# New places for the steps of the first third in a table-ordered kernel: attention front, its border to the second MLP pass, and that pass's first and last weight groups

## The chip, the cores and the metric

The kernel runs on one core of one Trainium2 chip. The metric is the device time of a run in microseconds (us), as the median of several runs. Five engines take part, each with its own instruction stream in program order: PE (TensorE: matrix multiplications and transposes), DVE (VectorE), ACT (ScalarE), POOL (GpSimd) and SP (SyncE, which here only issues DMA transfers). An engine starts an instruction when the one before it on the same engine allows it and when the semaphores named in its wait have reached their counts. ACT issues a few transfers too, and each of them stands in ACT's stream like any other instruction.

## The reference

```python
def phi(x):                                  # q and k: 4 batches, 8 heads, 576 rows, 64 columns
    proj = np.einsum('bhsd,df->bhsf', x, w_phi)              # w_phi: 64 x 128
    proj = proj - np.max(np.abs(proj), axis=-1, keepdims=True)
    return np.concatenate([np.exp(proj), np.exp(-proj)], axis=-1)
kv, z = einsum(k_p, v), sum(k_p)
x = (q_p @ kv) / (q_p @ z + 1e-06)           # linear attention, laid out as 2304 x 512
h = np.maximum(x @ moe_w_in, 0.0);  x = h * h @ moe_w_out              # 512 -> 2048 -> 512
p = probs / (probs.sum(-1, keepdims=True) + 1e-9)
out = sum over e of p[:, e:e+1] * (np.maximum(x @ w1[e], 0) @ w2[e])    # 4 experts, 512 -> 1024 -> 512
```

Everything is float32.

## The kernel before

**Arithmetic.** Most float32 products are made of three matmuls on a high part and a low part of each operand (`hi*hi + hi*lo + lo*hi`). So most operands need two more instructions: a copy that makes the high part (`copy`, L78 on ACT, L80 on DVE or POOL) and a subtraction that makes the low part (`sub`, L83 on DVE or POOL).

**Stages.** The attention works on 16 pairs of heads, `Pair(b, c)` with batch b and c from 0 to 3; P12 below is `Pair(1, 2)`. A pair loads q and k in three parts (`lqk`), transposes them on PE (`t_pe`), splits them (`t_hi` on ACT, `t_lo` on DVE), multiplies them with the split `w_phi` (`project`), shifts and exponentiates (`shift`, `exp_k`, `q_exp`), and forms the numerator (`num_pe` on PE, `num_out` on ACT). The denominator then makes two round trips through DRAM, all of them issued by SP: `den_put`, `den_get`, then `invert` on DVE, then `rec_put`, `rec_get`, and `divide` on DVE. The numerator's buffer exists once, so the next pair's `num_out` waits for this pair's `divide`.

Every product with `w_phi` needs the tile `wd`, which holds `w_phi` twice: `load_wd` loads one half by SP (L99) and the other by ACT (L100), and the step `split` makes `wd_h` and `wd_l` on DVE.

While the attention runs, the first MLP runs for batches 0 and 1, in `Unit` steps: U6b0 is weight group 6 of 8 on batch 0, with `hidden` (x @ w_in, L482), `relu`, `square`, the split of the result (`g_hi`, `g_lo`), and `out` 0 to 3 (L528, six matmuls each), whose results are summed by `add` (L536, DVE). `Matrix` steps turn the packed weights into float32 between them (`load`, `widen...`, `store`, `hi`, `lo`).

Then comes the border. Batches 2 and 3 take their MLP in a form with seven half-size products in place of eight. Its operands are sums of blocks of x: `Operands.load` (L1230, SP) fetches the x that P33, the last pair, has just stored (`put_x`, L387), and `Operands.sum` makes T3, T1, T2 and T4 on DVE (L83, 128x1024). `Rest` holds the rows left over from all batches; `Rest.make` splits them (ACT L78, DVE L83), and `RestUnit.hidden` (L1547) multiplies them. `PairUnit.product` (L1517) runs the seven products. Then follow the passes of the last stage, the mixture of experts, whose first weights are made in the last MLP group (575 to 625 us).

**Order.** Nothing in the loops decides the order. The table `PLACES` has one number for each call of each step; the function `at` takes the numbers of a step one after the other and sorts the calls by them, and this order is the order of the program on all engines:

```python
t = UNTIL * next(places["" if x is None else type(x).__name__, fn.__name__]) / STEPS
plan.append((t, len(plan), fn, args))
...
for _, _, fn, args in sorted(plan, key=lambda x: x[:2]):
    fn(*args)
```

For the pair steps with several calls the numbers run over the 16 pairs, and within a pair over the calls (for `t_pe` to `q_exp` these are columns 0 to 3, column 8, and columns 4 to 7 of nine).

Of the kernel before, what the change touches and what calls it, by code (L numbers as in the profile page):

```python
# [21 lines left out]
def fused_kernel(  # L22
# [515 lines left out]
    def new_x2(b):  # L538
# [12 lines left out]
            34, 1, 31,  # L551
        ),
        ("", "load_wd"): (
            2,
        ),
        ("", "split"): (
            3,
        ),
        ("Pair", "lqk"): (
            0, 13, 4, 25, 21, 50, 37, 41, 69, 71, 76, 80, 173, 168, 136, 185, 198, 145, 243, 233, 272, 294, 360, 297,  # L560
            388, 419, 367, 407, 573, 518, 508, 639, 583, 678, 618, 737, 828, 806, 855, 869, 964, 954, 916, 1182,
            1042, 1136, 1088, 1220,
        ),
        ("Pair", "lv"): (
            36, 35, 38, 78, 79, 53, 89, 43, 57, 154, 133, 195, 216, 237, 267, 271, 338, 290, 362, 372, 318, 425, 382,
            399, 549, 434, 569, 614, 501, 648, 740, 747, 780, 794, 887, 862, 1011, 1015, 944, 1123, 1106, 1195, 1298,
            951, 1301, 1189, 1200, 1023,
        ),
        ("Pair", "t_pe"): (
            5, 8, 14, 28, 56, 23, 40, 94, 92, 129, 115, 140, 179, 202, 201, 225, 261, 260, 278, 331, 329, 340, 353,  # L570
            395, 429, 397, 477, 458, 562, 574, 582, 626, 690, 686, 777, 772, 829, 913, 844, 930, 1052, 1062, 1127,
            1069, 1213, 1231, 1315, 1296,
        ),
        ("Pair", "t_hi"): (
            6, 9, 17, 42, 70, 29, 73, 97, 122, 135, 118, 142, 180, 208, 211, 230, 268, 275, 298, 332, 336, 341, 354,
            403, 440, 398, 480, 500, 566, 581, 594, 627, 693, 687, 779, 818, 858, 914, 845, 961, 1053, 1066, 1129,
            1087, 1214, 1232, 1319, 1304,
        ),
        ("Pair", "t_lo"): (
            7, 10, 20, 47, 72, 44, 87, 102, 126, 143, 119, 149, 193, 210, 212, 239, 269, 279, 310, 334, 337, 344,  # L580
            396, 414, 442, 411, 493, 516, 576, 592, 604, 628, 717, 688, 789, 819, 859, 920, 846, 1012, 1054, 1086,
            1145, 1125, 1259, 1233, 1352, 1305,
        ),
        ("Pair", "project"): (
            11, 16, 22, 48, 91, 63, 96, 116, 137, 161, 124, 172, 194, 221, 224, 253, 276, 292, 313, 335, 351, 377,
            402, 424, 445, 428, 522, 563, 577, 593, 653, 691, 718, 773, 821, 840, 878, 943, 980, 1019, 1075, 1094,
            1159, 1216, 1276, 1310, 1356, 1393,
        ),
        ("Pair", "shift"): (
            12, 26, 39, 49, 100, 64, 105, 127, 146, 165, 132, 184, 197, 238, 235, 258, 277, 293, 333, 342, 375, 409,  # L590
            413, 439, 483, 450, 543, 564, 589, 624, 677, 695, 739, 792, 822, 841, 927, 968, 997, 1073, 1084, 1140,
            1191, 1242, 1291, 1318, 1383, 1400,
        ),
        ("Pair", "exp_k"): (
            19, 27, 45, 67, 106, 101, 123, 128, 153, 183, 141, 189, 215, 244, 262, 282, 321, 339, 348, 343, 389, 447,
            415, 455, 506, 533, 555, 600, 590, 643, 745, 722, 752, 797, 871, 867, 966, 998, 1020, 1074, 1099, 1170,
            1253, 1267, 1306, 1360, 1401, 1412,
        ),
        ("Pair", "q_pe"): (
            18, 30, 54, 74, 107, 103, 144, 130, 160, 187, 156, 218, 214, 250, 273, 289, 285, 311, 347, 358, 386, 417,  # L600
            423, 469, 519, 536, 559, 605, 651, 655, 746, 714, 767, 823, 868, 910, 971, 977, 1007, 1133, 1144, 1143,
            1245, 1272, 1328, 1341, 1385, 1411,
        ),
        ("Pair", "q_exp"): (
            24, 32, 55, 81, 108, 111, 147, 169, 175, 188, 205, 223, 248, 257, 274, 304, 327, 328, 391, 380, 390, 418,
            463, 471, 521, 540, 572, 610, 652, 673, 750, 734, 775, 850, 870, 918, 972, 994, 1034, 1134, 1164, 1156,
            1246, 1273, 1333, 1357, 1408, 1419,
        ),
# [12 lines left out]
        ),  # L621
        ("Pair", "divide"): (
            157, 151, 219, 217, 283, 280, 349, 346, 421, 416, 468, 466, 539, 537, 607, 609, 704, 700, 847, 879, 1017,
            1006, 1155, 1161, 1275, 1280, 1363, 1365, 1436, 1435, 1489, 1490,
        ),
        ("Pair", "x_hi"): (
            200, 301, 314, 400, 443, 490, 591, 612,
        ),
        ("Pair", "x_lo"): (
            226, 326, 404, 460, 453, 561, 619, 623,  # L630
        ),
        ("Pair", "put_rest"): (
            220, 305, 352, 379, 454, 567, 662, 712, 778, 1137, 1103, 1201, 1418, 1406, 1439, 1501,
        ),
        ("Pair", "put_x"): (
            768, 1083, 1219, 1217, 1309, 1416, 1438, 1515,
        ),
        ("Matrix", "load"): (
            213, 15, 68, 361, 467, 492, 150, 596, 685, 731, 587, 835, 743, 813, 784, 946, 889, 978, 936, 1078, 1102,
            1190, 1013, 1205, 1209, 1324, 1149, 1355, 1295, 1404, 1392, 1493,  # L640
        ),
        ("Matrix", "widen"): (
            231, 33, 104, 401, 475, 534, 308, 646, 701, 732, 601, 836, 757, 890, 785, 981, 922, 1028, 952, 1079,
            1116, 1192, 1043, 1252, 1261, 1354, 1163, 1386, 1311, 1461, 1417, 1495,
        ),
        ("Matrix", "widen_power"): (
            284, 51, 174, 427, 498, 535, 309, 658, 707, 736, 602, 853, 764, 897, 790, 982, 923, 1029, 953, 1095,
            1117, 1193, 1048, 1254, 1262, 1359, 1180, 1394, 1312, 1464, 1426, 1508,
        ),
# [1364 lines left out]
```

## Time and profile before

| | before |
|---|---|
| runs shown | 1344.47, 1345.91 (median), 1347.03 us |
| profiled execution, device time | 1350.73 us |
| its span | 1349.0 us |
| PE busy in the span | 1321.6 us (98%) |
| DVE, POOL, ACT busy | 1043.0, 753.7, 698.2 us |

PE is the engine that is nearly always busy. Times in rows below are counted from the start of the span. The profiled execution took 4.82 us more than the median of the runs, and 1.73 us more than its own span.

### The profile page before, as it was taken

To read this page: it belongs to the slowest core of one execution; us is meant where nothing else is said; L and a number is where in the kernel's file an instruction comes from. 1 tells how busy PE (TensorE), PEld (TensorE's weight loads), DVE (VectorE), ACT (ScalarE), POOL (GpSimd) and SP (SyncE) were. 2 spreads that over 40 slices of the span, in tenths; PEclk is the share of its full clock that TensorE was granted. 3 is DMA by queue.
4 is the path that set the end of the run, shared out by engine and by line. 5 is a ranking of instruction groups with operands and counts; after the bars stand their busy time and mean duration, and the time that the engine had idled before them with its cause. 6 is when DMAs were issued, how large, how long until landed. Compare 5 with 4: busy or idle time off the path is not lost.

```text
span 1349.0 us, 19520 instructions
## 1 busy us (share of the span) xinstructions
PE 1321.6 (98%) x6945; PEld 1129.3 (84%) x6945; DVE 1043.0 (77%) x1525; ACT 698.2 (52%) x1165; POOL 753.7 (56%) x498
## 2 busy tenths in 40 slices
PE   9989999999989999999999999999999999999998
PEld 8989988888867888888888887887888888888886
DVE  6888777778785788998777676768787887878885
ACT  5676766566646666754233323425554454544542
POOL 4665444445446777879765656752454453445540
PEclk9999999999999999999999999999999999999999
DMA  5544554655372132125634545546546446445422
GB/s 134 123 107 133 146 156 135 180 144 163 103 240 81 63 105 68 64 94 206 230 126 142 217 175 183 201 159 186 173 149 191 144 128 196 142 144 158 155 94 78
DMA packets 169717, 196.16 MB, mean 145 GB/s; under 512 B 73916, under 2 KB 123012, under 8 KB 167572
## 3 DMA queue, kind: packets, MB, share of 16 engines
q1 hardware_dynamic: 167700, 192.39, 45.4%
q10 hardware_dynamic: 1920, 2.52, 0.5%
q8 instruction: 55, 0.90, 0.3%
q14 instruction: 42, 0.34, 0.1%
HBM read 130.72 MB, written 64.15 MB: 144 GB/s over the span
## 4 chain that ended last, share of the span: by engine, by line
PE 63%; DVE 4%; POOL 3%; DMA 1%; ACT 1%; issue 1%; DVEq 0%; ACTq 0%; SPq 0%; POOLq 0%
PE pa L1737 16%; PE px L1517 7%; PE pz L1517 7%; PE pv L1517 7%; PE pa L1633 7%; PE pa L1547 5%; PE py L1517 4%; PE pz L1633 2%; PE pv L1633 2%; PE px L1633 2%; PE pa L1710 2%; PE py L1633 1%; DMA x<-x 1%; PE pm L528 1%; POOL ol L83 1%
## 5 line engine op out<-in xcount | busy, mean ns | idle before, releaser
L83 POOL TENSOR_TENSOR gl<-u,gh 128x512 fp32r<-128x512 f32 x85 | 118.2, 1397 | 138.2 <-ACT gh L78 109.6
L1749 DVE SCALAR_TENSOR_TENSOR x<-pa,prob,x 128x512 f32<-128x512 f32 x150 | 109.5, 744 | 48.1 <-PE pa L1737 47.3
L78 ACT ACTIVATE w<-f 128x1024 fp32r<-128x1024 f32 x119 | 122.5, 1050 | 42.3 <-PE pv L1517 21.3
L1737 PE MATMUL pa<-w2l,gh 128*128 128x512 f32 x336 | 131.5, 391 | 2.1 <-DVE x L1749 0.9
L1737 PE MATMUL pa<-w2h,gl 128*128 128x512 f32 x336 | 131.0, 390 | 0.1
L1737 PE MATMUL pa<-w2h,gh 128*128 128x512 f32 x336 | 130.8, 389 | 0.0
L83 POOL TENSOR_TENSOR w<-f,w 128x1024 fp32r<-128x1024 f32 x41 | 105.8, 2590 | 36.5 <-ACT w L78 36.5
L83 POOL TENSOR_TENSOR w2l<-f,w2h 128x1024 fp32r<-128x1024 f32 x33 | 80.0, 2423 | 82.3 <-ACT w2h L78 80.2
L441 POOL TENSOR_TENSOR wf<-wf,power 128x512 f32<-128x512 f32 x32 | 42.0, 1312 | 104.3 <-DVE power L435 40.8
L1517 PE MATMUL pz<-oh,w 128*128 128x512 f32 x320 | 98.7, 390 | 0.0
L1517 PE MATMUL pv<-oh,w 128*128 128x512 f32 x320 | 98.7, 389 | 0.0
L1517 PE MATMUL px<-oh,w 128*128 128x512 f32 x320 | 98.6, 389 | 0.0
L1489 ACT ACTIVATE gh<-u 128x512 fp32r<-128x512 f32 x67 | 41.1, 626 | 96.2 <-DVE u L1527 71.2
L83 POOL TENSOR_TENSOR ql<-q,qh 128x1152 fp32r<-128x1152 f32 x32 | 85.9, 2693 | 8.2 <-ACT qh L78 7.3
L83 POOL TENSOR_TENSOR gl<-x,gh 128x512 fp32r<-128x512 f32 x45 | 61.9, 1384 | 46.4 <-ACT gh L78 44.5
L1310 POOL TENSOR_TENSOR f<-f 128x256 f32<-128x256 f32 x96 | 78.4, 837 | 14.4 <-DVE f L1348 4.9
L78 ACT ACTIVATE gh<-u 128x512 fp32r<-128x512 f32 x69 | 43.2, 627 | 82.5 <-DVE u L1591 81.6
L1737 PEld LDWEIGHTS pa<-w2l,gh 128*128 128x128 f32 x336 | 63.1, 188 | 16.5 <-DVE x L1749 1.4
L1547 PEld LDWEIGHTS pa<-rest,w 128*128 128x128 f32 x576 | 72.0, 191 | 5.3 <-DVE rest L83 3.6
L1527 DVE TENSOR_TENSOR u<-pz,u 128x512 f32<-128x512 f32 x80 | 55.0, 688 | 27.6 <-PE pz L1517 25.2
L1547 PE MATMUL pa<-rest,w 128*128 128x256 f32 x576 | 73.1, 283 | 2.8 <-DVE rest L83 2.8
L1737 PEld LDWEIGHTS pa<-w2h,gl 128*128 128x128 f32 x336 | 63.1, 188 | 13.8 <-DVE gl L1495 0.7
(250 smaller groups left out, 4057.7 us busy)
## 6 DMA issues: line engine op xcount, KB each, us to landing
f<-in_moe_w_dram SPq DMA_DIRECT2D x96, 256.0 KB
f<-l SPq DMA_DIRECT2D x47, 512.0 KB
l<-w SPq DMA_DIRECT2D x16, 1024.0 KB
s<-f SPq DMA_DIRECT2D x31, 512.0 KB
f<-s SPq DMA_DIRECT2D x31, 512.0 KB
raw<-in_moe_w_out_dram SPq DMA_DIRECT2D x16, 512.0 KB
raw<-in_moe_w_in_dram SPq DMA_DIRECT2D x16, 512.0 KB
f<-in_moe_w_dram SPq DMA_DIRECT2D x64, 128.0 KB
```

The lines of the kernel that those rows point to most:

```text
L78: nc.scalar.activation(out=dst, in_=src, func=AF.Copy)
L83: eng.tensor_tensor(out=dst, in0=a, in1=b, op=ALU.subtract)
L441: nc.gpsimd.tensor_tensor(out=self.dst, in0=self.dst, in1=f32(self.power), op=ALU.mult)
L1310: nc.gpsimd.tensor_tensor(out=s[:, i], in0=a, in1=b, op=op)
L1489: nc.scalar.activation(out=self.gh, in_=self.r, func=AF.Copy if self.square else AF.Relu)
L1517: nc.tensor.matmul(p, lhsT=a, rhs=m, start=start and i == 0, stop=i == len(ops) - 1, skip_group_check=not start)
L1527: nc.vector.tensor_tensor(out=self.u[out], in0=self.p[a], in1=self.u[b], op=ALU.add)
L1547: nc.tensor.matmul(q, lhsT=a[:, s, k], rhs=m[:, kk], start=kk + j == 0, stop=kk == KD - 1 and j == 2)
L1633: nc.tensor.matmul(self.p[b, d], lhsT=a, rhs=m, start=start and i == 0, stop=i == 2, skip_group_check=not start)
L1710: nc.tensor.matmul(self.p[:, :n], lhsT=a, rhs=m, start=i == 0, stop=i == len(ops) - 1)
L1737: nc.tensor.matmul(self.p, lhsT=a, rhs=m, start=i == 0, stop=i == len(ops) - 1)
L1749: nc.vector.scalar_tensor_tensor(out=o, in0=p, scalar=pe, in1=o, op0=ALU.mult, op1=ALU.add)
```

## The change

Only numbers in `PLACES` change: those of the steps up to about place 1810 (the attention, the units of batches 0 and 1, the border and the first weight groups of batches 2 and 3) and from about 2150 to 2510 (the last MLP group and the first weights of the experts). The instructions are the same ones. Two of the entries, of some hundred:

```diff
         ("", "load_wd"): (
-            2,
+            4,
         ),
         ("Pair", "t_hi"): (
-            6, 9, 17, 42, 70, 29, 73, 97, 122, 135, 118, 142, 180, 208, 211, 230, 268, 275, 298, 332, 336, 341, 354,
...
+            3, 8, 21, 40, 77, 45, 59, 97, 117, 137, 123, 149, 180, 243, 196, 231, 256, 277, 283, 340, 338, 354, 393,
...
```

What the numbers do is seen in the order of instructions. The first place is the head of ACT's stream. `qk` is the tile of the first pair's q and k, `th` the high part of their transpose, `wd` the tile for `w_phi`. Before:

```order
1 L154 DMA qk<-in_k_dram 128x4x64
2 L100 DMA wd<-in_w_phi_dram 64x128 [waits DVE_49]
3 L78 ACT_TABLE_LOAD
4 L78 ACTIVATE th<-pa 128x512 [waits PE_49]
5 L78 ACTIVATE th<-pa 128x128 [waits PE_49]
```

And now:

```order
1 L154 DMA qk<-in_k_dram 128x4x64
2 L78 ACT_TABLE_LOAD
3 L78 ACTIVATE th<-pa 128x512 [waits PE_49]
4 L100 DMA wd<-in_w_phi_dram 64x128 [waits DMAHW7_49,DVE_49]
5 L78 ACTIVATE th<-pa 128x128 [waits PE_49]
```

ACT's half of `load_wd` has gone behind the first `t_hi`, and it has a wait that it did not have: DMAHW7 is the semaphore of the transfer that brings the second half of the first pair's k. That transfer is the seventh in SP's stream now, because SP issues the first weight load of the MLP (`raw`, L406, 128x1024) ahead of it:

```order
2 L99 DMA wd<-in_w_phi_dram 64x128 [waits DVE_49]
3 L152 DMA qk<-in_q_dram 128x1x64
4 L152 DMA qk<-in_k_dram 128x1x64
5 L406 DMA raw<-in_moe_w_out_dram 128x1024
6 L154 DMA qk<-in_q_dram 128x4x64
7 L154 DMA qk<-in_k_dram 128x4x64
```

Before, row 5 here stood behind rows 6 and 7.

The second place is DVE's stream at the border. `f<-x_3` is T3, `x_3<-x_3,x_2` is T1, the second `f<-x_3` is T2; L536 is an `add`, L506 a `square`, `gl` a `g_lo`. Before:

```order
450 L536 TENSOR_TENSOR x_0_144<-pm,x_0_144 128x512 [waits PE_49]
451 L506 SCALAR_TENSOR_TENSOR ph<-ph,r 128x512 [waits DVE_49,Activation_49]
452 L83 TENSOR_TENSOR f<-x_3_4904 128x1024 [waits DMAHW1_49,DMAHW0_49]
453 L83 TENSOR_TENSOR x_3_4904<-x_3_4904,x_2_4903 128x1024 [waits DMAHW2_49,DVE_49]
454 L536 TENSOR_TENSOR x_0_144<-pm,x_0_144 128x512 [waits PE_49]
455 L83 TENSOR_TENSOR gl<-ph,gh 128x512 [waits Activation_49]
456 L506 SCALAR_TENSOR_TENSOR ph<-ph,r 128x512
457 L83 TENSOR_TENSOR f<-x_3_4904 128x1024 [waits DVE_49]
```

And now:

```order
452 L506 SCALAR_TENSOR_TENSOR ph<-ph,r 128x512 [waits DVE_49,Activation_49]
453 L536 TENSOR_TENSOR x_0_144<-pm,x_0_144 128x512 [waits PE_49]
454 L83 TENSOR_TENSOR f<-x_3_4910 128x1024 [waits DMAHW3_49,DMAHW2_49]
455 L83 TENSOR_TENSOR x_3_4910<-x_3_4910,x_2_4909 128x1024 [waits DMAHW4_49,DMAHW0_49,DVE_49]
456 L506 SCALAR_TENSOR_TENSOR ph<-ph,r 128x512 [waits Activation_49]
457 L536 TENSOR_TENSOR x_0_144<-pm,x_0_144 128x512 [waits PE_49]
458 L83 TENSOR_TENSOR gl<-ph,gh 128x512 [waits Activation_49]
459 L83 TENSOR_TENSOR f<-x_3_4910 128x1024 [waits DVE_49]
```

One more `square` (row 456) stands between T1 and the first `g_lo` of U7b0. On PE, at the same border, `out` 1 of U6b0 has moved down behind `hidden` 0 of U7b0, next to `out` 0; PE's last work before it needs that `g_lo` is `out` 2 of U6b0 in both orders. P33's last `num_pe`, on which the stored x depends, has 12 matmuls fewer ahead of it in PE's stream (2022 instead of 2034).

The third place is PE's stream where the rest rows begin. `px` and `pv` are products of the pair (x B21 and v T4), L528 an `out`. Before, the last six rows ahead were `out` 3 of U7b0:

```order
1873 L528 MATMUL pm<-gl,wh 128x512
1874 L528 MATMUL pm<-gh,wl 128x512
1875 L528 MATMUL pm<-gh,wh 128x512
1876 L1547 MATMUL pa<-rest,w_4911 128x256 [waits DVE_49]
1877 L1547 MATMUL pa<-rest,w_4911 128x256 [waits Activation_49]
```

And now:

```order
1874 L528 MATMUL pm<-gh,wh 128x512
1875 L1517 MATMUL px<-ol,w_4924 128x512
1876 L1517 MATMUL px<-oh,w_4924 128x512 x2
1877 L1517 MATMUL px<-ol,w_4924 128x512
1878 L1517 MATMUL px<-oh,w_4924 128x512 x2
1879 L1517 MATMUL pv<-ol,w_4924 128x512 [waits Pool_49]
1880 L1517 MATMUL pv<-oh,w_4924 128x512 [waits Activation_49]
1881 L1517 MATMUL pv<-oh,w_4924 128x512
1882 L1517 MATMUL pv<-ol,w_4924 128x512
1883 L1517 MATMUL pv<-oh,w_4924 128x512 x2
1884 L1547 MATMUL pa<-rest,w_4924 128x256 [waits DVE_49]
```

Twelve matmuls of two products have moved in between.

## Rows read from the trace of the kernel before

**Rows 1.** The page, part 1: busy time, share, instructions.
```profile
PE 1321.6 (98%) x6945; PEld 1129.3 (84%) x6945; DVE 1043.0 (77%) x1525; ACT 698.2 (52%) x1165; POOL 753.7 (56%) x498
```

**Rows 2.** PE's waits by releaser: us in total, times, longest us.
```profile
PE pm L528 <- DVE gl L83: 5.0, 1, 5.0
...
PE pp L242 <- DVE tl L83: 2.2, 3, 1.2
```

**Rows 3.** Stretches: length, then busy us of PE, PEld, DVE, ACT, POOL; clock.
```profile
50.00:125.00 75.00, 69.51 (x539) 64.83 (x537) 60.03 (x86) 52.40 (x130) 49.41 (x28) 1.00 0.47 123
385.50:390.50 5.00, 0.00 (x0) 0.00 (x0) 4.97 (x5) 2.60 (x4) 2.62 (x2) 0.99 0.29 82
390.50:394.00 3.50, 3.50 (x9) 2.78 (x10) 2.81 (x4) 3.50 (x5) 2.63 (x1) 0.53 1.05 382
```

**Rows 4.** Timeline of ACT, head: start, us, instruction, idle before and its releaser.
```profile
1.47 0.63 ACTq L100 DMA_DIRECT2D wd<-in_w_phi_dram  x1
...
5.32 0.60 ACT L78 ACTIVATE th<-pa 128x512 fp32r<-128x512 f32 x1 [1.91 <-PE pa L212]
```

**Rows 5.** Timeline of SP, head.
```profile
4.30 0.72 SPq L154 DMA_DIRECT2D qk<-in_k_dram  x1
5.06 0.62 SPq L406 DMA_DIRECT2D raw<-in_moe_w_out_dram  x1
```

**Rows 6.** Timeline of DVE, head.
```profile
4.84 0.29 DVE L80 CAST wd_h<-wd 128x256 fp32r<-128x256 f32 x1 [3.70 <-DMA wd<-in_w_phi_dram]
...
5.95 0.69 DVE L83 TENSOR_TENSOR tl<-pa,th 128x512 fp32r<-128x512 f32 x1 [0.36 <-ACT th L78]
```

**Rows 7.** Timeline of PE, head: first product, its last one, and the next transposes.
```profile
6.75 0.56 PE L242 MATMUL pp<-wd_h,tl 128*128 128x256 f32 x1
...
8.75 0.28 PE L244 MATMUL pp<-wd_h,th 128*128 128x256 f32 x1
8.87 0.60 PE L212 MATMUL pa<-ident,qk 128*128 128x128 f32 x4
```

**Rows 8.** Timeline of DVE and PE, in the attention front.
```profile
50.21 0.22 DVE L348 RECIPROCAL rec<-rec 128x9 f32<-128x9 f32 x1 [0.37 <-DMA rec<-den]
...
51.02 0.38 PE L242 MATMUL pp<-wd_h,tl 128*128 128x256 f32 x1 [0.81 <-DVE tl L83]
...
89.02 0.35 PE L328 MATMUL pm<-qh,zh 128*65 128x288 f32 x1 [1.30 <-ACT num L335]
```

**Rows 9.** Timeline of PE near 250 us.
```profile
250.75 0.35 PE L242 MATMUL pp<-wd_h,tl 128*128 128x256 f32 x1 [1.19 <-DVE tl L83]
```

**Rows 10.** Timeline of SP and DVE at the border: x loads, add, T3, T1, g_lo, T2.
```profile
376.13 2.65 SPq L1230 DMA_DIRECT2D x<-x  x4
...
381.43 0.69 DVE L536 TENSOR_TENSOR x<-pm,x 128x512 f32<-128x512 f32 x1 [1.19 <-PE pm L528]
...
384.06 3.00 DVE L83 TENSOR_TENSOR f<-x 128x1024 f32<-128x1024 f32 x1 [1.14 <-DMA x<-x]
387.08 2.17 DVE L83 TENSOR_TENSOR x<-x,x 128x1024 f32<-128x1024 f32 x1
...
389.78 0.67 DVE L83 TENSOR_TENSOR gl<-ph,gh 128x512 fp32r<-128x512 f32 x1
...
390.97 1.21 DVE L83 TENSOR_TENSOR f<-x 128x1024 f32<-128x1024 f32 x1
```

**Rows 11.** Timeline of POOL at the border.
```profile
386.02 2.15 POOL L83 TENSOR_TENSOR wl<-wf,wh 128x512 fp32r<-128x512 f32 x1
```

**Rows 12.** Timeline of PE in the rest rows and the last group.
```profile
411.44 0.39 PE L528 MATMUL pm<-gl,wh 128*128 128x512 f32 x1
...
412.58 0.39 PE L528 MATMUL pm<-gh,wh 128*128 128x512 f32 x1
415.42 1.82 PE L1547 MATMUL pa<-rest,w 128*128 128x256 f32 x13 [2.45 <-DVE rest L83]
...
622.32 0.50 PE L1737 MATMUL pa<-w2l,gh 128*128 128x512 f32 x1 [0.58 <-POOL w2l L83]
```

More of the change, by code (lines that the diff above doesn't have):

```diff
@@ L624, in fused_kernel @@
-            1006, 1155, 1161, 1275, 1280, 1363, 1365, 1436, 1435, 1489, 1490,
+            152, 153, 214, 212, 287, 294, 350, 355, 411, 412, 466, 465, 540, 543, 614, 615, 702, 719, 853, 852, 1021,
+            1037, 1160, 1172, 1275, 1276, 1353, 1359, 1423, 1421, 1494, 1495,
         ),
         ("Pair", "x_hi"): (
-            200, 301, 314, 400, 443, 490, 591, 612,
+            174, 292, 346, 383, 522, 500, 555, 622,
         ),
         ("Pair", "x_lo"): (
-            226, 326, 404, 460, 453, 561, 619, 623,
+            219, 295, 365, 421, 565, 520, 587, 624,
@@ L699, in fused_kernel @@
+            1170, 1331, 1261, 1335, 1350, 1462, 1487, 1453, 1468, 1549, 1511, 1518, 1556,
         ),
         ("Unit", "out"): (
[4 rows of a table removed]
[4 rows of a table added]
         ),
         ("Unit", "add"): (
[4 rows of a table removed]
[4 rows of a table added]
         ),
         ("", "open_early"): (
-            1524,
+            1527,
         ),
         ("", "open_late"): (
-            1608,
+            1609,
         ),
         ("", "load_probs"): (
-            1657,
+            1662,
         ),
         ("Operands", "load"): (
-            1538, 1547, 1534, 1536,
+            1535, 1537, 1530, 1533,
@@ L905, in fused_kernel @@
         ("Spread", "out"): (
-            1672,
+            1675,
         ),
         ("Spread", "put"): (
-            1674,
+            1680,
         ),
         ("MlpWeights", "load"): (
-            1525, 1612, 1659, 1733, 1868, 1921, 2039, 2121,
+            1528, 1610, 1670, 1733, 1868, 1921, 2039, 2121,
         ),
         ("MlpWeights", "load2"): (
-            1586, 1649, 1719, 1834, 1915, 2032, 2104, 2228,
+            1551, 1574, 1645, 1834, 1915, 2032, 2104, 2215,
         ),
         ("MlpWeights", "sums"): (
-            1527, 1624, 1695, 1756, 1869, 1982, 2040, 2131,
+            1529, 1631, 1701, 1767, 1869, 1982, 2040, 2131,
@@ L928, in fused_kernel @@
         ),
         ("MlpWeights", "hi2"): (
-            1604, 1653, 1742, 1876, 1941, 2071, 2111, 2233,
+            1565, 1587, 1758, 1876, 1941, 2071, 2111, 2218,
         ),
         ("MlpWeights", "lo"): (
-            1531,
+            1539,
         ),
         ("MlpWeights", "lo2"): (
-            1616,
+            1603,
         ),
         ("MlpWeights", "load_lo"): (
-            1631, 1660, 1815, 1871, 1956, 2019, 2133,
+            1619, 1640, 1815, 1871, 1956, 2019, 2133,
         ),
@@ L941, in fused_kernel @@
         ("MlpWeights", "load2_lo"): (
-            1555, 1743, 1842, 1901, 1959, 2129, 2218,
+            1557, 1761, 1842, 1901, 1959, 2129, 2253,
         ),
         ("MlpWeights", "lo_kept"): (
-            1632, 1707, 1836, 1922, 1981, 2092, 2184,
+            1628, 1696, 1836, 1922, 1981, 2092, 2203,
         ),
         ("MlpWeights", "lo2_kept"): (
-            1596, 1744, 1849, 1964, 2037, 2169, 2227,
+            1584, 1766, 1849, 1964, 2037, 2163, 2254,
         ),
         ("MlpWeights", "sums2"): (
-            1665, 1757, 1838, 1937, 2033, 2115,
+            1630, 1746, 1838, 1937, 2033, 2115,
```

226 lines of the change are left out of this document (112 added, 114 removed), and 108 rows, old and new, of the table PLACES.

## The prediction

> **What bounds the kernel now.** I read the page first: PE is busy 98% of the span [rows 1], 1349.0 − 1321.6 = 27.4 us idle. Nothing but those 27 us, and stretches in which PE runs at its lower clock, can be won by a new order of the same instructions; what can be lost has no such limit. So the next views are PE's waits and, for the stretches that the change touches, the timelines of PE and of whoever releases it. The reader is to see four places.
>
> The head: PE's first real product starts at 6.75 [rows 7], released by a chain that runs over ACT's transfer of half of `w_phi` (issued at 1.47 [rows 4]), the cast on DVE at 4.84 and `t_lo` at 5.95 [rows 6].
>
> The attention front: from 50 to 125 us PE is busy for 69.51 of 75 us [rows 3], 5.5 us idle, mostly for `t_lo` on DVE and `num_out` on ACT [rows 2, 8].
>
> The border: PE does nothing from 385.5 to 390.5 and then works for 3.5 us at a mean granted clock of 0.53, which is its lower level (1.2 of 2.4 GHz) for nearly all of the stretch [rows 3].
>
> The rest rows: 2.45 us idle at 415.42 [rows 12].
>
> **The change, part by part.** Times are on the clock of the profiled execution before, 1350.73 us. A delay at the head shifts everything behind it alike, so later terms are worked out as if there were none.
>
> *Head.* ACT's load of `w_phi` now waits for the second half of the first k. That transfer was issued at 4.30; with the weight load ahead of it, whose issue takes SP 0.62, it goes at about 4.95 [rows 5]. From issue to first use the load of `w_phi` took 4.84 − 1.47 = 3.37 [rows 4, 6]; the same time brings k at 8.3. Then ACT issues, and 3.37 later, at 11.7, the cast can start. From the cast to the first product before were 6.75 − 4.84 = 1.91, of which 0.36 was DVE's wait for the high part [rows 6], which is long there now: 1.55, so the product starts at 13.2 and not at 6.75, **+6.5**. PE has nothing else to do meanwhile: what stood behind the products (more transposes, the warming-up transposes) still does. Upper bound: the transposes of that k began 8.87 − 4.30 = 4.57 after its issue [rows 5, 7], an upper bound on its landing; with that the head costs +7.7. Lower bound: if the wait were met early, ACT could issue once its copy ends at 5.32 + 0.60 = 5.92 [rows 4], and the product would start at 5.92 + 3.37 + 1.55 = 10.8, +4.1.
>
> The clock comes on top. Before, the twelve products took 8.75 − 6.75 = 2.00 us between first and last start, where eleven steps at the last one's 0.12 take 1.32 [rows 7]: 0.7 lost. After the 5.0 us of nothing at the border, 3.5 us at 0.53 lost 3.5 × 0.47 = 1.65 [rows 3]. PE now idles for about 6 us before the products, so I take the border's price: 1.65 − 0.7 = +1.0 (0 to 1.65). **Head: +7.5**, bounds +4.1 and +9.3. Nothing later gives it back: PE's next products, the first numerator and all later pairs hang on these.
>
> The Trainium skill speaks against this part: "DMA: Bandwidth & Descriptors", section "Rules for kernel authors", says to issue a transfer early and to wait for it late. The section "Anatomy of one DMA" there puts a GpSimd-issued transfer at about 2.0 us plus its bytes at 436 GB/s. By an estimate from that page, `w_phi`'s 32 KB take 2.1 us and k's 128 KB 2.3, the first product would start near 10.9, and the sum below would be some 2.3 lower. The row of this very load shows 3.37, so I go by the row.
>
> *Front.* P10's first `t_lo` stood behind P01's `invert`, which waited 0.37 for a transfer at 50.21, and PE then waited 0.81 for it at 51.02 [rows 8]; now it stands ahead of that `invert`. The puts and gets of P03's and P10's denominators follow each other directly on SP, where other loads stood between; P03's `divide`, and so the next numerator, whose wait at 89.02 was 1.30 [rows 8], can come earlier. Against that, P12's and P13's `project` of columns 8 and 4 to 7 still stand close behind `t_lo`s, and P01's `rec_get` and P02's `rec_put` have loads ahead of them on SP that wait for PE. The bounds: at best nearly all of the 5.5 idle [rows 3] goes, −5; at worst two more waits of the kind of 0.81 and 1.30 come, +2. I take **−2.5**, a little under half of the idle time, since the two waits that the order clearly frees make 2.1.
>
> *Near 250 us.* P31's `t_lo` no longer queues behind P22's `divide`: −1.19 [rows 9]. But an `out` of U3b0 has moved 6.8 us of PE's work forward and now waits for a weight's low part from POOL. No row prices that; bounds are 0 and the wait it replaces doubled. I take the same 1.19: **0**, ±1.2.
>
> *Border.* P33's last `num_pe` comes 12 matmuls earlier. Five steps between matmuls of 128x512 take 412.58 − 411.44 = 1.14 us [rows 12], so 12 take 2.7. T3 waited until 384.06 for the stored x, 1.14 of it idle [rows 10]; so x is there at 381.4. DVE's queue now has U6b0's `add` ahead of T3, which could start at 381.43 before and still can, since PE's `out` 0 keeps its place. It takes 0.69, so T3 runs from 382.1 and takes 3.00 to 385.1. T1 took 2.17 and T2, the same operation later, 1.21 [rows 10]; T1 had POOL's 2.15 us subtraction beside it [rows 11], which it will meet again in part: I take 1.7, to 386.8. Then come the added `square` and the `add`, 0.6 each from start to start (from `g_lo` to T2 there are two such steps, 390.97 − 389.78 = 1.19), and `g_lo` 0.67 [rows 10]: 388.7, where it was 389.78 + 0.67 = 390.45. **−1.75**. Bounds: T1 at 1.21 gives −2.2; T3 starting as late as before gives +0.2.
>
> PE's idle time is then 3.2 us. After 5.0 the clock fell [rows 3]; the 2.45 before the rest rows is the nearest shorter one, and the 13 matmuls behind it run at 1.82 / 13 = 0.14 each [rows 12], the full clock's pace for 256 columns against 0.23 for 512. 3.2 lies nearer to 2.45, so I take it that the clock stays: **−1.65** (bound 0).
>
> Rest rows: 12 matmuls of two products now stand before their first matmul, 2.7 us [rows 12]. The wait there was 2.45: **−2.6** with the gap's start counted from matmul to matmul (415.42 − 412.58 − 0.23), bound −1.5 if the moved product waits for its own operand from POOL. New small waits at the border: an `out` behind T2 and `g_lo` on DVE, 1.21 + 0.67 = 1.9 behind the first, with 1.4 of PE's work in between, +0.5, and that operand, +0.3: **+0.8** (0 to 2). The border sums to **−5.2**.
>
> The rule that bears on T1 stands in "SBUF — State Buffer" of the Trainium skill, section "Who interferes with whom": a DVE instruction with two SBUF inputs contends with a GpSimd instruction that reads SBUF, and whoever starts first has the port for its whole instruction. T3 and T1 against T2 fit the first half. If POOL always began first, T1 would lose the full 0.96 again, and the sum would be 0.5 higher.
>
> *Last group.* Its first product waited 0.58 for POOL's low part at 622.32 [rows 12], and steps of POOL move ahead there: **−0.5** (−1.5 to +0.5).
>
> Sum: 7.5 − 2.5 + 0 − 5.2 − 0.5 = −0.7. The profiled execution would take 1350.0; its 4.82 above the median stay, so the median becomes **1345.2**.
>
> **The rivals.** *The gap at the border stays (slower).* If SP issues the x loads no earlier, because other transfers ahead of them hold its stream, T3 starts at 384.06 again, and with the added `square` ahead of it `g_lo` ends at 384.06 + 3.0 + 2.0 + 0.6 + 0.6 + 0.67 = 390.9. The idle time is 5.4, the clock falls, and the border gives only −2.6 + 0.8 + 0.4 = −1.4. Sum +3.1: 1349.0. It decides from a T3 start of about 383.5 on. For it speaks that four loads of x and three of weights share SP with the put [rows 10]; against it that the whole chain moved.
>
> *The front loses (slower).* The two unfreed kinds of wait outweigh: +2 in place of −2.5, sum +3.8: 1349.7. For it: loads that wait for PE now stand ahead of denominators on SP.
>
> *The head costs less (faster).* The lower bound, +4.1: sum −4.1, 1341.8. For it: 3.37 was measured while several transfers started at once; against it, a 512 KB load is now in flight ahead of k.
>
> *The front pays in full (faster).* −5: sum −3.2, 1342.7. For it: every listed wait there is shorter than 1.5 us; against it, the waits that remain are of the same kind.
>
> **Chances and range.** Two runs must differ by about 0.2% (2.7 us) to be told apart here, so "same" is 1343.2 to 1348.6. My forecast 0.40 (own range 1342.2 to 1348.2: same 0.26, faster 0.08, slower 0.06); the border gap 0.20 (slower 0.14, same 0.06); the front's loss 0.10 (0.08, 0.02); the cheap head 0.16 (faster 0.13, same 0.03); the front in full 0.14 (0.11, 0.03). Together faster 0.32, same 0.40, slower 0.28. The range reaches from below the cheap head with a good front, 1339.5, to above the lost front, 1351.5.
>
> **What would show each step.** Head: PE's first product at 13.2 and DVE's cast at 11.7, with the waits put down to the `w_phi` transfer. Front: less than 5.5 idle in its 75 us, and no 0.81 before P10's products. Border: T3 about 2 us earlier against PE's last `out`, an idle time near 3.2 and a granted clock of 1.0 behind it; no wait for `rest`. The prediction is wrong if the first product starts before 11 or after 15, if the clock at the border falls again, or if the front's idle time grows.

## The result, and the profile after

The changed kernel is slower: 1352.15 us (median of 6 runs, 1351.18 to 1356.47) against 1345.74 (6 runs, 1344.03 to 1347.03) for the kernel before beside it. The ratio is 1.0054, 95% interval 1.0039 to 1.0070. A ratio here is worked out from all runs and differs a little from that of the medians, which lie 6.4 us apart; 0.54% would be 7.3 us. The prediction, 1345.2 with a range to 1351.5, was wrong, and "slower" had the smallest of its three chances.

The profiled execution after took 1351.18 us, of which 1349.4 are its span; I had put that one at 1350.0. Of the miss of 6.95 us in the median, 1.2 lie in the sum. The other 5.8 lie in what was added to it: the profiled execution of before stood 4.8 above its median, that of after stands 1.0 below. How the miss divides depends on the execution: a second profile of the changed kernel (e14 below) took 1353.64, and against that one 3.6 lie in the sum.

First the page of the kernel after, part 1 (busy time, share, instructions), to be held against [rows 1]: PE is 2.2 us less busy in a span 0.4 us longer.

```profile
PE 1319.4 (98%) x6945; PEld 1128.7 (84%) x6945; DVE 1035.4 (77%) x1525; ACT 699.6 (52%) x1165; POOL 753.1 (56%) x498
```

PE's waits after, by releaser (us in total, times, longest); [rows 2] are those of before.

```profile
PE pp L242 <- DVE tl L83: 6.6, 1, 6.6
PE pm L328 <- ACT num L335: 3.3, 3, 1.3
PE pm L528 <- DVE gl L83: 3.1, 2, 1.6
...
PE pa L1547 <- DVE rest L83: 1.8, 2, 1.5
```

The 5.0 at the border is gone, replaced by two waits that make 3.1; 2.5 before the rest rows has become 1.5; and the first line is new.

That first line is the head. Timelines after, of SP, ACT, DVE and PE in this order (start, us, instruction, idle before and its releaser):

```profile
3.41 0.47 SPq L406 DMA_DIRECT2D raw<-in_moe_w_out_dram  x1
...
4.55 0.63 SPq L154 DMA_DIRECT2D qk<-in_k_dram  x1
```
```profile
5.50 0.60 ACT L78 ACTIVATE th<-pa 128x512 fp32r<-128x512 f32 x1 [2.75 <-PE pa L212]
9.08 0.55 ACTq L100 DMA_DIRECT2D wd<-in_w_phi_dram  x1
9.67 0.28 ACT L78 ACTIVATE th<-pa 128x128 fp32r<-128x128 f32 x1 [3.57 <-DMA qk<-in_k_dram]
```
```profile
11.85 0.29 DVE L80 CAST wd_h<-wd 128x256 fp32r<-128x256 f32 x1 [10.71 <-DMA wd<-in_w_phi_dram]
```
```profile
13.26 0.58 PE L242 MATMUL pp<-wd_h,tl 128*128 128x256 f32 x1 [6.61 <-DVE tl L83]
...
15.78 0.41 PE L244 MATMUL pp<-wd_h,th 128*128 128x256 f32 x1
```

ACT could have issued at 6.10, when its copy ended, and issued at 9.08, 4.53 after the issue of the k that it waits for. The cast stood at 11.85 (11.7 forecast), the first product at 13.26 (13.2 forecast).

Stretches after (length, busy us of PE, PEld, DVE, ACT, POOL, granted clock, DMA share, GB/s): the head's products, the front, the place near 250 us, and the border with the rest rows.

```profile
13.26:16.30 3.04, 3.04 (x14) 3.04 (x15) 0.89 (x4) 0.00 (x0) 0.00 (x0) 0.51 0.00 0
50.00:125.00 75.00, 68.16 (x558) 65.33 (x557) 55.28 (x82) 50.23 (x126) 49.70 (x29) 1.00 0.51 119
225.00:260.00 35.00, 35.00 (x204) 30.54 (x204) 26.36 (x45) 21.11 (x42) 15.86 (x11) 1.00 0.57 172
375.00:425.00 50.00, 45.38 (x208) 36.60 (x207) 40.54 (x47) 26.08 (x35) 28.13 (x20) 1.00 0.52 171
```

The products at the head run at the lower clock (0.51, 1.2 of 2.4 GHz) after 6.6 us of waiting. PE is idle for 6.84 of the front's 75 us, more than the 5.5 of [rows 3]; the prediction had named that as a sign that it would be wrong. Near 250 us PE has no idle time at all, where [rows 9] had 1.19. At the border the clock is 1.00 throughout.

The border after, on DVE (add, T3, T1, square, add, g_lo, T2, g_lo), with POOL's subtraction that lies beside T2, and PE's waits:

```profile
387.54 0.69 DVE L536 TENSOR_TENSOR x<-pm,x 128x512 f32<-128x512 f32 x1
388.30 1.69 DVE L83 TENSOR_TENSOR f<-x 128x1024 f32<-128x1024 f32 x1
390.02 1.23 DVE L83 TENSOR_TENSOR x<-x,x 128x1024 f32<-128x1024 f32 x1
...
392.36 0.68 DVE L83 TENSOR_TENSOR gl<-ph,gh 128x512 fp32r<-128x512 f32 x1
392.96 3.42 DVE L83 TENSOR_TENSOR f<-x 128x1024 f32<-128x1024 f32 x1
396.30 0.68 DVE L83 TENSOR_TENSOR gl<-ph,gh 128x512 fp32r<-128x512 f32 x1
```
```profile
392.88 2.42 POOL L83 TENSOR_TENSOR w<-f,w 128x1024 fp32r<-128x1024 f32 x1
```
```profile
393.10 0.50 PE L528 MATMUL pm<-gl,wh 128*128 128x512 f32 x1 [1.52 <-DVE gl L83]
397.03 0.50 PE L528 MATMUL pm<-gl,wh 128*128 128x512 f32 x1 [1.60 <-DVE gl L83]
```

T3 waits for no load any more. T3 and T1 are shorter than in [rows 10], T2 much longer: POOL's subtraction had begun 0.08 us ahead of it, and T2 ended 1.08 behind POOL's end.

### The profile page after: what moved, and what is told of

It is laid out like the page before. It is cut to its first block, busy times and chain, and to the rows that moved or that the text cites. A ratio compares the mean times of both kernels' runs of the same rounds, so it can differ in the third digit from the quotient of the medians.

```text
span 1349.4 us, 19461 instructions
## 1 busy us (share of the span) xinstructions
PE 1319.4 (98%) x6945; PEld 1128.7 (84%) x6945; DVE 1035.4 (77%) x1525; ACT 699.6 (52%) x1165; POOL 753.1 (56%) x498
## 3 DMA queue, kind: packets, MB, share of 16 engines
q10 hardware_dynamic: 1920, 2.52, 0.5%
## 4 chain that ended last, share of the span: by engine, by line
PE 90%; DVE 4%; DMA 3%; SPq 2%; ACT 1%; issue 1%; DVEq 0%; ACTq 0%
PE pa L1737 16%; PE pz L1517 8%; PE px L1517 8%; PE pv L1517 8%; PE pa L1633 7%; PE ph L482 6%; PE pm L528 6%; PE pa L1547 5%; PE py L1517 4%; PE pa L1710 3%; PE pa L309 2%; PE pa L328 2%; PE px L1633 2%; PE pz L1633 2%; PE pv L1633 2%; PE py L1633 1%
```

## The experiments

Two theories stood against each other. The first: the head costs about 7 us, nothing gives it back, and the gap of 5.0 at the border of before was a chance of one execution, so that there was less to win than the sum had it. The rival: that gap is in every run of before and its gain is real, and some other part of the change, or the new work around it, loses what is missing. Each edit is in `PLACES`.

**e1_before_again: the kernel before, unchanged, with a second profile.**

> The kernel before once more, for its profile. Theory A: the execution profiled first (1350.73 us) lost some 5 us that its usual runs (1345.7) do not lose, at the border: then the gap before U7b0's first out is under 2 us here, the clock does not fall behind it, and the execution takes 1344 to 1347. Rival B: the gap of 5.0 us and the lower clock belong to every run of the kernel before, and the 5 us lie elsewhere or are the profiled execution's own: then gap and clock repeat here.

1348.44 us. Its waits of PE, then T3 and T1 on DVE, then the border's stretch and the one behind the gap:

```profile
PE pa L1547 <- DVE rest L83: 2.8, 2, 2.5
...
PE pm L528 <- DVE gl L83: 2.1, 1, 2.1
```
```profile
382.24 2.44 DVE L83 TENSOR_TENSOR f<-x 128x1024 f32<-128x1024 f32 x1
384.72 1.23 DVE L83 TENSOR_TENSOR x<-x,x 128x1024 f32<-128x1024 f32 x1
```
```profile
387.90:391.50 3.60, 3.60 (x11) 2.78 (x10) 3.57 (x4) 3.60 (x5) 3.03 (x2) 0.56 0.93 308
375.00:425.00 50.00, 45.42 (x196) 37.35 (x195) 32.73 (x40) 27.53 (x39) 31.39 (x21) 0.93 0.57 185
```

The same program has a gap of 2.1 where [rows 2] had 5.0. The difference lies in loads that landed later, and in what POOL did with them. POOL in the first profile of before, and then in e1 (sums of the weights `w_i`, then a subtraction):

```profile
380.67 2.95 POOL L1310 TENSOR_TENSOR f<-f 128x256 f32<-128x256 f32 x4 [1.73 <-DMA f<-w_i]
383.58 2.39 POOL L83 TENSOR_TENSOR w<-f,w 128x1024 fp32r<-128x1024 f32 x1
```
```profile
378.31 2.94 POOL L1310 TENSOR_TENSOR f<-f 128x256 f32<-128x256 f32 x4 [0.57 <-DMA f<-w_i]
381.21 2.40 POOL L83 TENSOR_TENSOR w<-f,w 128x1024 fp32r<-128x1024 f32 x1
```

In the first profile POOL waited 1.73 for `w_i`, which SP issues just ahead of x, and T3 waited 1.14 for x [rows 10]; in e1 the waits were 0.57 and none. In both, POOL's subtraction began ahead of T3, and T3 ended about 1.1 behind its end (387.06 behind 385.97, 384.68 behind 383.61). So T3's end follows POOL's subtraction, and through it the landing of `w_i`. T1 then began ahead of POOL's next subtraction in e1 (384.72, POOL's at 385.63) and took 1.23; in the first profile it began 1.06 behind it and took 2.17 [rows 10, 11]. Why the loads landed later in one execution is not known. The parts "under 2 us", "the clock does not fall" and "1344 to 1347" of theory A were missed: the gap was 2.1, the clock fell behind it, and the time was 1348.44. PE's busy time over 375 to 425 us, 45.42, is that of the changed kernel, 45.38; what the changed order is better by there, against this execution, is the clock, 1.00 against 0.93.

**e2_after_early_wd: the changed kernel with `load_wd` at its first place again.**

```diff
         ("", "load_wd"): (
-            4,
+            1.5,
```

> The changed kernel with one number undone: load_wd ahead of the first transposes again, so that ACT's half of w_phi is issued before its first copy. Theory A (the head costs 6.5 to 7.5 us and nothing gives it back): 6.5 to 7.5 below the changed kernel, so about 1345 and within 1.5 us of the kernel before. Rival (the delay at the head is largely absorbed by the loop of the denominators later in the front): less than 3 below the changed kernel, over 1349.

1347.05 us (12 runs) against 1347.46 (17): 1.0002, 0.9989 to 1.0016. One step put back takes all of the loss away. The k behind the 512 KB load is still late: PE's next transposes wait 0.62 and 1.05 us for k.

**e3_before_late_wd: the kernel before with only this step late (and `split`, which needs it).**

```diff
         ("", "load_wd"): (
-            2,
+            6.5,
...
         ("", "split"): (
-            3,
+            6.6,
```

> The kernel before with that one part of the change alone: load_wd behind the first t_hi, so that ACT's half waits for the second part of the first k. Theory A: 6 to 7.5 us slower than before (no 512 KB load stands ahead of k here, so the wait is some 0.5 shorter), 1352 to 1353. Rival (absorbed later): less than 3 slower.

1354.17 us (6 runs) against 1347.46: 1.0053, 1.0038 to 1.0068. The medians lie 6.7 us apart, the whole of what the change costs. The first product, its stretch and the border:

```profile
12.84 0.58 PE L242 MATMUL pp<-wd_h,tl 128*128 128x256 f32 x1 [6.65 <-DVE tl L83]
```
```profile
12.84:15.56 2.72, 2.72 (x12) 2.72 (x13) 0.14 (x1) 0.00 (x0) 0.00 (x0) 0.50 0.00 0
375.00:425.00 50.00, 45.30 (x208) 36.85 (x207) 36.76 (x48) 24.79 (x35) 28.47 (x20) 1.00 0.64 202
```

The clock falls here too, at the head. At the border this execution, in the order of before, waits 1.6 at most for a `g_lo` and has a clock of 1.00, as the changed kernel has.

**e7_all_but_head: the changed kernel with the first 17 steps in the order of before.**

```diff
         ("", "load_wd"): (
-            4,
+            2,
...
         ("Matrix", "load"): (
-            200, 13, 50, 351, 436, 490, 284, 641, 668, 661, 584, 821, 752, 837, 811, 963,
+            200, 15, 50, 351, 436, 490, 284, 641, 668, 661, 584, 821, 752, 837, 811, 963,
```

> The changed kernel with the first 17 steps of before: load_wd, and also the weight load that had gone ahead of k, as before. Theory A: head as before, front within 0.5, the place near 250 us 1.3 faster, border 2.5, last group 1.4: 4 to 5 us below before, some 11 below the changed kernel. The prediction's sizes: 8.2 below before. Rival: like the run with load_wd alone undone, within 1.5 of before.

1345.31 us (11 runs) against 1346.59 (23): 0.9993, 0.9984 to 1.0001. All the rest of the change is worth 0.9 us by the ratio (1.3 between the medians), with no change at the edge of the interval. By the prediction's terms (−2.5, 0, −5.2, −0.5) it should have been 8.2, by theory A 4 to 5; the rival held.

**e14_after_again: the changed kernel, unchanged, a second time.**

> The changed kernel once more, on the chip of the others. Theory C: 6 to 7 us slower than before, and its border shows the same three waits near 1.5 us as in its first profile. Rival: the waits at its border vary from run to run as those of before do.

1353.64 us (5 runs): 1.0055, 1.0043 to 1.0067. The first product was at 13.93 after a wait of 6.9; the border's waits were 1.5, 1.6 and 1.5 again.

**e4_border_alone, e5_border_blend, e13_border_cut: only the border's order changed.** e4 keeps the first 1400 steps of before, e13 the first 1520, and e5 passes over little by little. In all three:

```diff
         ("Operands", "load"): (
-            1538, 1547, 1534, 1536,
+            1535, 1537, 1530, 1533,
```

> The order of before for the first 1400 steps (head and front), then the changed order of all remaining steps (border, last group). Theory A: the border of before costs its usual runs little, so this is 0 to 2 us faster than before. Rival B (the sum of the prediction): 5.7 us faster, 1340.

> The border and the last group alone, with a smooth passage: the order of before up to about place 1150, the changed order from 1500 on, and between them each step at a place that slides from the one to the other. Theory A (sizes read from the profiles of the changed kernel and of the kernel before run again): border 2.5 and last group 1.4 faster, 3 to 4 us below before. The prediction's own sizes: 5.7 below. Rival (the changed border gains nothing against the usual runs of before): 0 to 1.5 below.

> The order of before for the first 1520 steps, then the changed order; at this cut 2 steps differ, so that the passage costs nothing: the changed border (without P33's earlier numerator) and last group alone. Theory C: border 2, last group 1.2 below the usual runs of before, together 3. The prediction's own terms: 5.7 less what P33's 12 matmuls bring, 4 to 5. Rival: no gain, because before's usual border is no worse than the changed one.

e4: 1354.77 us, 1.0056 (1.0040 to 1.0072); e5: 1360.34, 1.0098 (1.0083 to 1.0112). Neither total says anything about the border, since the passage from one order to the other made waits of its own (in e4, some 9 us of lost time at 349 to 363 us). Inside both, the border lost what it loses in the changed kernel. e13 has no such passage: 1347.49, 1.0005 (0.9996 to 1.0014). But it keeps P33's last numerator at its old place, and there T3 waits for x again. DVE, PE and the stretch behind the gap in e13:

```profile
382.15 3.11 DVE L83 TENSOR_TENSOR f<-x 128x1024 f32<-128x1024 f32 x1 [1.59 <-DMA x<-x]
385.30 2.17 DVE L83 TENSOR_TENSOR x<-x,x 128x1024 f32<-128x1024 f32 x1
```
```profile
389.32 0.80 PE L528 MATMUL pm<-gl,wh 128*128 128x512 f32 x1 [5.41 <-DVE gl L83]
```
```profile
389.30:393.00 3.70, 3.68 (x9) 2.91 (x10) 2.79 (x4) 3.70 (x5) 3.60 (x2) 0.50 0.00 0
```

Here too POOL waited for `w_i`, 2.44 us, and with the loads late T3, T1 and the gap take the lengths of [rows 10] and [rows 2]. So the new order on DVE does not take the gap away by itself. The earlier numerator brings P33's store of x, and the loads of `w_i` and x behind it on SP, forward. In the ten profiles with it (after, e2, e4, e5, e7, e9 to e12, e14) T3 never waits for x and the gap is 1.5; in the seven without it (before, e1, e3, e6, e8, e13, e15) the gap is 1.6 to 5.4. That fits the earlier numerator as what makes the border steady; no run moves it alone, so it is not shown. The 3 us that theory C gave e13 did not come.

**e6_last_group_alone: only the places from 2000 on.**

```diff
         ("Operands", "sum"): (
-            1537, 1540, 1550, 1580, 2191, 2212, 2239, 2299, 3078, 3079, 3122, 3151,
+            1537, 1540, 1550, 1580, 2189, 2207, 2229, 2294, 3078, 3079, 3122, 3151,
```

> The changed order of the last MLP group and the first expert weights alone (places from 2000 on), all else as before. Theory A: 1.4 us faster, because the wait of 0.58 for POOL's low part at 622 and three smaller waits go. The prediction's size: 0.5. Rival: nothing, since the work behind waits for POOL anyway.

1345.77 us (12 runs) against 1346.59: 0.9996, 0.9985 to 1.0007. Too small to measure; in its profile the 0.58 of [rows 12] is gone.

**e8_front_alone, e12_front_of_before, e15_front_cut: the front by itself.** e8 has the changed front and passes over to the old order little by little; e12 has the first 600 steps of before and then the changed order; e15 has the changed order in steps 18 to 600 alone. Of e15:

```diff
         ("Pair", "lqk"): (
-            0, 13, 4, 25, 21, 50, 37, 41, 69, 71, 76, 80, 173, 168, 136, 185, 198, 145, 243, 233, 272, 294, 360, 297,
...
+            0, 13, 4, 23, 27, 55, 39, 54, 61, 75, 74, 109, 147, 135, 177, 170, 242, 224, 270, 247, 293, 320, 291,
```

> The changed front alone: first 17 steps as before, then the changed order up to about place 1150, sliding back to the order of before by 1500. Theory A: the front moves waits and gains nothing, near 250 us 1.3 are won: 0.5 to 2 us below before. The prediction's size: 2.5 below. Rival (the front loses, by its bound): 2 above.

> The order of before for the first 600 steps (head and attention front), then the changed order; at this cut only 8 of the 600 steps differ between the two orders. Theory C (the changed front itself loses about 2 us where the head is early): 2 us below the run with only the head undone, 3 to 4 below before. Rival (the front costs the same in both orders): as that run, 1 below before.

> The changed front alone: steps 18 to 600 in the changed order, the rest as before. Theory C: 2 us slower than before. The prediction's term: 2.5 faster. Rival: no difference.

e8: 1364.26 us, 1.0133 (1.0120 to 1.0146), again by waits of its passage at 300 to 370 us. e12: 1347.81, 1.0008 (0.9999 to 1.0017), not the 3 to 4 below before that theory C gave it; its front loses nothing, but its passage has a wait of 2.3 at 155 us. e15: 1349.85 (8 runs) against 1346.97 (25): 1.0030, 1.0019 to 1.0040. The changed front by itself is a loss, of 2.9 us between the medians (4.0 by the ratio). Its stretch has 7.0 us without PE, the place of [rows 3] 5.5:

```profile
50.00:125.00 75.00, 68.00 (x535) 64.44 (x535) 54.39 (x82) 47.91 (x122) 48.14 (x29) 1.00 0.50 122
```

Where it comes from is read in the kernel after, from SP (P02's `rec_put` and `rec_get`), DVE (P01's and P02's `divide`) and PE:

```profile
72.23 0.57 SPq L351 DMA_DIRECT2D den<-rec  x1
75.61 0.49 SPq L355 DMA_DIRECT2D recs<-den  x1
```
```profile
62.85 1.52 DVE L362 TENSOR_TENSOR x<-num,recs 64x576 f32<-64x576 f32 x2 [0.90 <-DMA recs<-den]
...
79.85 1.51 DVE L362 TENSOR_TENSOR x<-num,recs 64x576 f32<-64x576 f32 x2 [1.79 <-DMA recs<-den]
```
```profile
81.95 0.35 PE L328 MATMUL pm<-qh,zh 128*65 128x288 f32 x1 [1.27 <-ACT num L335]
```

From put to get are 3.38 us (1.41 before, 65.31 to 66.72). Two loads now stand between them on SP; they are issued by 74.06, and the get then waits 1.55 more for the put to land. Why the put lands later is not shown: with the get directly behind it (e9, next) they are still 2.15 apart. From P01's to P02's divide are 17.0 (14.25 before, 56.70 to 70.95); DVE waits 1.79 for the result, and PE behind it for the numerator.

**e9_rec_get, e10_glo_before_T2, e11_both: two mends on e7.** e9 puts that `rec_get` directly behind its `rec_put`; e10 puts U7b1's second `g_lo` ahead of T2; e11 has both.

```diff
         ("Pair", "rec_get"): (
-            128, 206, 274, 330, 410, 464, 517, 608, 701, 851, 1020, 1127, 1270, 1337, 1408, 1477,
+            128, 206, 261, 330, 410, 464, 517, 608, 701, 851, 1020, 1127, 1270, 1337, 1408, 1477,
...
         ("Operands", "sum"): (
-            1538, 1541, 1553, 1571, 2189, 2207, 2229, 2294, 3078, 3079, 3122, 3151,
+            1538, 1541, 1556, 1571, 2189, 2207, 2229, 2294, 3078, 3079, 3122, 3151,
```

> The kernel with all of the change but the head (e7), and P02's rec_get directly behind its rec_put on SP, as it was before the change; in e7 two loads of q and k stand between, and P02's divide ends its round 17.2 us after P01's, where it was 14.3 before. Theory (the changed front loses about 2 us to this one transfer): PE's waits for num_out of P03 and for the transposes of P12 shrink, the front ends 1 to 2 us earlier than in e7, and the time is 1 to 2 below e7. Rival (the loads of q and k were needed there; PE waits for them instead): no gain.

> As e7, with one swap on DVE at the border: the second g_lo of U7b1 ahead of T2. Theory (T2 met POOL's subtraction and took 3.4 instead of 1.2, and PE waited 1.57 for the g_lo behind it): that wait goes to under 0.2, 1.0 to 1.6 below e7. Rival (the work moves to T2's own reader, the product y): the wait comes back there, no gain.

> Both edits, as a candidate that beats both kernels: if they add, 2 to 3.5 us below e7, so 3 to 5 below before, about 1342.

e9: 1348.31 us, 1.0011 (1.0002 to 1.0019); e10: 1346.40, 1.0005 (0.9994 to 1.0017); e11: 1347.95, 1.0014 (1.0005 to 1.0022). No mend is a gain, so the theories of all three failed. PE in e9 and in e10:

```profile
73.62 0.63 PE L212 MATMUL pa<-ident,qk 128*128 128x128 f32 x4 [3.51 <-DMA qk<-in_k_dram]
```
```profile
388.75 0.50 PE L528 MATMUL pm<-gl,wh 128*128 128x512 f32 x1 [1.52 <-DVE gl L83]
396.01 0.50 PE L528 MATMUL pm<-gl,wh 128*128 128x512 f32 x1 [1.52 <-DVE x L536]
```

In e9 that wait for the numerator is gone and the loads that `rec_get` has overtaken are late, 3.51 us; in e10 the second wait is about as long but has another releaser, an `add` that stands behind T2 and a low part of 2.83 us on DVE. None of the runs made for this study beats the kernel before beyond its interval; e7 comes nearest.

## Why the prediction was wrong

**The step that failed: "its 4.82 above the median stay".** I took the excess of one profiled execution as a constant beside the change. It was not. Beside the changed kernel and the experiments the kernel before ran 98 times: median 1346.8, from 1343.5 to 1350.9, and only two of the 98 took longer than 1350.73. Being profiled is not what cost it: the fifteen other profiled executions that have runs of their kernel beside them lie between 1.2 below and 1.9 above those runs' medians. Part of that excess was the very thing which the change replaces: 5.0 us of waiting at the border and 1.65 at half clock [rows 3], of which the same program shows 2.1 in e1; other executions with that border show 2.2 (e6), 1.8 (e15) and 1.6 (e3). A gain worked out against it is no gain against an ordinary run. In terms of the sum, held against three other executions in the order of before (end of this section), the border's −5.2 was −1.3 and the front's −2.5 was +0.8, 7.2 us together. The table shows it by stage. It is worked out from PE's timelines: for each instruction the time to the next one's start, less the median of that for its kind in the first profile of before; summed over the stretch that does the same PE work; as difference from that first profile, in us.

| execution | head | front | 250 us | border | after it | sum | device time − 1350.73 |
|---|---|---|---|---|---|---|---|
| forecast for the change | +7.5 | −2.5 | 0 | −5.2 | −0.5 | −0.7 | |
| after | +7.0 | +0.4 | −1.5 | −3.7 | −1.8 | +0.4 | +0.45 |
| after, e14 | +8.5 | +1.6 | −1.5 | −3.8 | −1.9 | +2.9 | +2.91 |
| before, e1 | −0.7 | +0.2 | +0.2 | −1.5 | −0.6 | −2.3 | −2.29 |
| before, late `wd`, e3 | +7.9 | +0.6 | −0.8 | −4.2 | −0.5 | +2.9 | +2.93 |
| before, last group, e6 | −0.1 | −0.3 | −0.9 | −1.7 | −0.2 | −3.1 | −3.03 |
| all but head, e7 | −0.1 | +1.8 | −1.5 | −3.8 | −1.9 | −5.5 | −5.42 |

Three executions with the border of before (e1, e3, e6) lie 1.5 to 4.2 us below the first profile there, and e3 even below the changed order. That the sum on the first profile, −0.7, came out at +0.4 is in part luck: the front and the border gave 2.9 and 1.5 less than forecast, the head, the place near 250 us and the stretch behind the border 0.5, 1.5 and 1.3 more.

**Head: right.** +7.5 forecast, +7.0 and +8.5 in the two profiles of the changed kernel; the step alone costs 6.7 us (e3) and nothing gives it back (e2, e7). The first product came 6.51 us later for +6.5, and that close a hit is luck. Three errors nearly cancel: k was issued at 4.55 and not at 4.95, took 4.53 from issue to ACT's release and not 3.37 (the upper bound had 4.57), and `w_phi` took 11.85 − 9.08 = 2.77 and not 3.37. In e14 k took 4.52 and `w_phi` 3.18; in e3, with no 512 KB load ahead of k, 3.08 and 3.79. The clock fell, 0.51 over 3.04 us, but the twelve products took 15.78 − 13.26 = 2.52 from first to last start, 0.5 more than in [rows 7], where 1.0 was taken. In e14 the clock was at 0.50 from 14 to 19 us, which goes with its +8.5. The clock's part also differs between runs: two of the six runs of the changed kernel had a mean granted clock of 1.000 and took 1351.2 and 1351.8, the profiled one 0.997 and 1351.18. The prediction's estimate from the Trainium skill's "DMA: Bandwidth & Descriptors", section "Anatomy of one DMA" (first product near 10.9), was 2.4 too early. The same page of the Trainium skill says in "Rules for kernel authors" to issue a transfer early; e2 and e3 agree: late, it costs 6.7 us.

**Front: the sign was wrong.** −2.5 forecast; the profiles show +0.4 to +1.8, and e15 alone a loss of 2.9 us in its runs, of which its profile shows about 1.0 in the front; where the other part lies was not found. I had counted the waits that the order frees (the 0.81 of [rows 8] did go) and set the loads ahead of the `rec_get` down as a bound. The numerator exists in one buffer, so that round trip holds up the next pair's numerator: 17.0 us from divide to divide for 14.25, and 3.3 us of PE's waits for `num_out` for 2.0.

**Near 250 us: better than forecast.** The wait of 1.19 went and nothing came in its place (−1.5). Against ordinary executions this is −1.0, for that wait varied too: 1.4 in e1, 0.4 in e3, 0.3 in e6, all in the order of before.

**Border: the direction right, the size and part of the mechanism not.** On the first profile it gave −3.7 for −5.2. T3 began 0.76 behind the start of the `add` ahead of it, about as reckoned, and without a wait for x. T3 took 1.69 for my 3.00: I had read 3.00 as its length, but POOL's subtraction had held it, begun 0.48 ahead of it there and 1.80 here. T1 took 1.23 for my 1.7. But T2 took 3.42 for 1.21: the wait I had priced at 0.5 was 1.60. The one before it was 1.52 (3.2 was taken), and the one before the rest rows stayed at 1.50 (I had it gone). So PE idles 4.6 in all, as in e1 with 2.1 + 2.5. What remains against e1, e6 and e15 is the clock: it fell there (0.93 over 375 to 425 us) and in neither profile of the changed kernel, but not in e3 either, which has the order of before. My reading that it stays because 3.2 is nearer to 2.45 than to 5.0 had no ground: in e1 it fell after 2.1, in e15 after 1.8.

**Last group: more than forecast**, −1.8 for −0.5, though e6 cannot tell it from nothing in the runs.

Of the rivals, "the front loses" came true; "the gap at the border stays" did not in the changed kernel, but in e13, where x is late. Against the other executions in the order of before (means of e1, e3 and e6, without e3 at the head and without e6 behind the border, where they are changed), the two profiles after give +8.1 at the head, +0.8 in the front, −1.0 near 250 us, −1.3 at the border and −1.3 behind it: +5.3, where the runs gave 6.4 (7.3 by the ratio).

## What to carry to other kernels

Before a gain is worked out from a wait in one profile, see whether that execution is an ordinary one of its runs, and take a second profile if it isn't: a wait that comes and goes pays for nothing. A delay ahead of the first product of the engine that bounds the kernel was paid in full here: by one step out of several thousand the first product came 6.1 us later in e3, and the runs took 6.7 longer. When a step is moved ahead on a queue, price what it overtakes: both mends here turned one wait into another. When an instruction's length is taken from a row, see what ran beside it: of T3's 3.00 and T1's 2.17 some 1.8 and 0.9 were spent on POOL, against the 1.2 of T2 in the same profile.

## What the runs showed of the hardware

**One program, two borders.** In all seventeen profiles T3 ended 1.08 us (once 1.09) behind the end of POOL's 128x1024 subtraction, which had begun before it. In the order of before, T3 and T1 took 3.00 and 2.17 us when POOL waited 1.73 for its load, and 2.44 and 1.23 when it waited 0.57 (e1). Some 1.2 us more of waiting for a transfer went with 2.9 more of PE's idle time.

**DVE beside POOL.** T2 took 1.21 in the first profile of before [rows 10], where POOL's next instruction began 0.40 behind it (391.37), and 3.42 in the kernel after, where POOL had begun 0.08 us earlier; it then ended 1.08 behind POOL's end. T1 of [rows 10] ended 1.08 behind POOL's subtraction of [rows 11] too. The same is seen at another place of the kernel after, where POOL began 0.02 ahead (DVE's row is shown first):

```profile
411.28 2.91 DVE L1485 TENSOR_TENSOR u<-u 128x512 f32<-128x512 f32 x1
```
```profile
411.26 2.38 POOL L83 TENSOR_TENSOR ol<-f,oh 128x1024 fp32r<-128x1024 f32 x1
```

The Trainium skill's "SBUF — State Buffer", section "Who interferes with whom", says that a DVE instruction with two SBUF inputs contends with a GpSimd instruction that reads SBUF, that the port pair they share is an exclusive lock, and that the order of issue decides who blocks. These rows agree, with 0.55 us (128x512) and 1.08 (128x1024) left after POOL's end. POOL first, the case that the prediction only mentions, is what lengthened T2.

**The clock.** In the order of before PE's granted clock fell from its upper level (2.4 GHz) to 0.53 behind the 5.0 us of waiting in the first profile, to 0.56 behind 2.1 in e1 and to 0.50 (390 to 392 us) behind 1.8 in e15. It did not fall behind 1.6 in e3, nor behind the 1.5 and 1.6 that followed each other within 4 us in the kernel after. Before the rest rows the wait of 2.5 us was followed by a lower clock in e1, e6 and e15 (24 matmuls took 4.64, 4.43 and 4.63) and not in the first profile and e3 (3.14 in both). The length of the wait alone does not tell which it will be. The runs suggest what this is worth: of the 92 runs of before beside the experiments, the 56 with a mean granted clock of 0.999 or more took 1346.1 us on average, the 27 with 0.997 or less 1348.6. The execution profiled first had 0.999 and 1350.73, 2.1 above the slowest of those 56, so its excess was more waiting than clock.
